# Another order of the same instructions, from the first scores on, in a fused attention and SoLU kernel

## The chip, the core and the metric

The kernel runs on one core of a Trainium2 chip. The metric is device time in microseconds (us) per execution. A program for this core is five streams of instructions that run side by side and meet at semaphores: TensorE (PE in the profile) multiplies matrices, VectorE (DVE) and ScalarE (ACT) work elementwise and read its results from PSUM, GpSimd (POOL) works on SBUF, and SyncE (SP) issues transfers. Each stream runs in the order in which it is written.

## The reference

A cluster-routed attention over 4 batches, 8 heads, 768 tokens and 64 dimensions, and a feed-forward layer with a SoLU activation and a layer norm on its 3072 tokens:

```python
def _attn_ref(q, k, v, centroids):
    q_assign = np.argmax(np.einsum('bhsd,hcd->bhsc', q_n, c_n), axis=-1)
    k_assign = np.argmax(np.einsum('bhsd,hcd->bhsc', k_n, c_n), axis=-1)
    mask = q_assign[:, :, :, None] == k_assign[:, :, None, :]
    scores = np.where(mask, scale * (q @ k.transpose(0, 1, 3, 2)), -1000000000.0)
    return softmax(scores) @ v

def _moe_ref(x, w_in, w_out, g_ln):          # x: 3072 x 512, w_in: 512 x 1024
    h = x @ w_in
    solu = h * softmax(h)
    ln = (solu - mean(solu)) / sqrt(var(solu) + 1e-06) * g_ln
    return ln @ w_out
```

Here `q_n`, `k_n` and `c_n` are rows divided by their norms, and there are 16 centroids for each head.

## The kernel before

**Attention.** The work goes by pairs of heads: 4 batches with 4 pairs each, 16 pairs in all, written b.p below (the second pair of batch 0 is 0.1). For one pair SyncE loads the rows of q and k (`raw`, L406, or L381 in a few pairs) and v (`vf`, L536). They are turned so that the dimensions lie on the partitions (`xt`: on VectorE at L414, or on TensorE at L393 with a copy at L400). TensorE multiplies them with the centroids: 8 matmuls into one PSUM buffer make a cluster-score group (`csc`, L452 and L457). VectorE takes the maximum (L479) and makes a one-hot row of the cluster (`oht`, L491 to L501). GpSimd casts q and k to bf16 (L440, L442) into the pair's place in `qk` and copies the one-hot rows beside them (L513 and L523; L532 blanks the rest), so that one product gives the score and the mask together.

There are six places (`slot`), used in turn, so copies, casts and blanks of a pair wait for the scores of the pair six before it, and the scores of a pair wait for its copies. TensorE then multiplies in banks of 512 columns (`sps`, L615, two matmuls in a bank). A bank lies in one of three PSUM buffers that are used in turn, and ScalarE's exponential (`e`, L625) empties it. A value group is six matmuls with `v` (`ops`, L644) into one of six places of an output bank. When such a bank is full, VectorE takes the reciprocal of the sums (L656) and scales (L669) into `x`. There is one such bank, so the next value group waits for that division.

**Feed-forward.** It goes by row tiles of 128 tokens, 24 in all, f = 0 to 23. SyncE transposes `x` by a transfer (L704). TensorE computes h in four parts of two 512-column matmuls (`hreg`, L736). VectorE takes the maximum (L742), ScalarE the exponential (L748), VectorE the product with h (`u`, L755). SyncE transposes `u` (L760), VectorE makes the statistics (L766, L770), GpSimd a factor alpha from them (L776, L782, L785). TensorE multiplies with the output weights (`yps`, L800, eight 512-column matmuls), and VectorE or ScalarE scales the result by alpha (L817), after which SyncE stores it (L827). `hreg` has three banks, of which even row tiles use the first two and odd ones the last two. A single PSUM buffer serves both the cluster-score groups and y, so each of these waits for whoever emptied it last.

**What sets the order.** The class `Weave` holds the whole program as operations with names, kinds and needs. `ORDER` (L28 to L78) gives for each of the five engines a list of kinds in which a number repeats the kind before it: `S` a score bank, `V` a value group, `h` one of the four parts of a row tile's h, `y` one of the parts of its y, `cl` a cluster-score group, `ca`, `cv`, `pl` and `bl` casts of q and k, casts of v, copies of one-hot rows and blanks, `al` and `at` steps of alpha, `ld` and `lv` loads, `tx`, `tu` and `ou` the transfers of x, u and the output, `ex` the exponential of h, `N` a division. `queues` takes, for each entry, the next operation of that kind that is written for that engine, so operations of one kind never pass each other:

```python
for kind, n in re.findall(r"([A-Za-z]+)(\d*)", text):
    for _ in range(int(n or 1)):
        queues[e].append(of[e, kind].pop(0))
```

`run` walks the five lists together to a plan of start times and writes the instructions out by them; what each engine runs, and in what order, is fixed by its list. `AWAY` says which operations run on another engine than their default.

Of the kernel before, what the change touches and what calls it, by code (L numbers as in the profile page):

```python
# [22 lines left out]
class Weave:  # L23
# [5 lines left out]
    ORDER["SP"] = """
        ld4 si ld4 lg lv ld2 lv ld3 lo ld lv ld2 lv ld2 lo2 ld3 lo ld4 li ld li3 tx ld lv  # L30
        ld3 lv tx ld3 tu ld8 tu tx ld5 lv tu ld3 ou ld3 tu ou ld2 lv ld10 tu ld6 ou tx lv
        ld2 tu ld ou ld2 tx ld tu ld2 lv ld2 tx ld tu ou2 ld lv ld8 tu2 ld ou ld7 pl ou ld
        lv2 ld3 tu lv tx ou tu lv pl ld4 ou2 tx lv tu tx ou tu pl2 tu2 tx tu tx ou2 tx ou tu
        tx2 ou tu2 ou2 tu2 ou6
    """
    ORDER["POOL"] = """
        po zo ca3 z ca pl ca bl pl2 ca bl ca pl sg cv z ca3 cv ca pl cv pl2 ca2 pl gs pl2 cv
        ca z ca z2 cv ca2 pl3 ca2 pl cv pl3 ca bl ca wi4 cv at ca2 pl2 cv ca pl ca pl cv al
        at2 ca cv bl ca al ca pl al pl bl pl cv at pl ca4 at ca2 al ca pl2 bl pl2 cv2 ca3 al
        at pl2 bl pl2 ca pl al ca3 at cv at pl ca pl2 ca2 pl al cv2 bl cv2 pl2 ca pl al pl  # L40
        at al at pl2 ca3 at al bl cv pl2 bl cv2 ca3 pl5 al cv3 at al ca2 cv ca cv ca2 at ca2
        pl ca al pl2 at2 pl3 at ca cv al at2 al2 at2 al at al3 at al2 at2 al2
    """
    ORDER["PE"] = """
        fl wm fl tp2 cp fl2 cl tp fl tp fl4 cl S3 tp2 S cq tp S tp S tp S2 tp S tp S2 cl S2
        tp S V S V S V S gt V S V2 S cl S3 V3 S tp S tp S tp S2 tp V S V2 S2 cl S4 V S V3 S3
        V S V S V S V S cl S3 V3 S2 V S su S4 V2 S V S V su S4 V2 S V S V me S4 V2 ptx V2 S4
        cl S2 V2 S h S V S V S h3 S2 V2 S V S2 V h2 V S V S V S h S V S h S3 V S h S V3 h S
        V2 S h S h S2 y S y2 S y S V S V S V cl h S V S h S2 V2 S h2 S3 y4 V2 h V S V S h S
        V h V S h2 S y3 S2 y V3 h S3 cl V2 S V S y S2 y2 S3 V3 S y S2 V3 S2 cl S V S2 V2 S h  # L50
        S2 V2 S V S h S2 V2 cl V2 S3 y2 S V S2 V y S2 y V2 S3 h2 S V h S h S2 V h S V S V y2
        S h V y2 S2 V S h3 S cl V S2 V2 S h V cl S3 h2 V y V S3 y2 V S h V3 S y S h S2 h2 S3
        V2 y h S V S2 y V3 y S3 h3 y S3 V3 S h S V S V cl S V S h S cl V2 S3 y V2 S y S2 y
        V2 S3 h y V S3 V h V2 S3 cl S2 V2 S y3 S2 y S V3 S V S y S2 V S V3 S2 y2 S3 y V2 S2
        h V2 S3 h3 S V S2 V y S V h2 V2 S y S2 y V y S h2 S3 cl h V S2 V3 S h V2 S3 h2 S y
        S2 V h S2 V y2 V4 S3 y h S2 h V h V S V S y2 S3 V3 h2 S2 h2 S2 y2 S V S h2 S V3 S2 h
        S h S2 V S y V2 S V y2 S2 h2 S2 h2 V2 S2 V2 y S2 h V2 h V S2 h S V h S3 V2 h y S V
        y3 V h3 S2 y3 S2 y h2 V2 h y h y3 h V h V y4 h ptx h y4 h2 y3 h2 y ptu2 y6 ptu y ptu
        y5
    """  # L60
    ORDER["DVE"] = """
        cn xa cb ca tb mx oh ot pl2 tb mx oh ot xa3 cf xa2 ca cv tb xa mx oh gk N ot pl tb
        xa mx xa oh xa ot N xt pl N tb mx xt cv N oh ot tb mx pl N oh ot ca N xt sk N ce xt
        tx ce N ce2 tb ce2 N ce hm ce N u mx bn oh N hm ot xt u bn2 ag N hm xt sc xt tb u
        bn2 N hm mx bn ag oh u ot xt ag N cv bn hm bn ag sc xt2 tb mx N u xt oh ot sc N bn2
        xt ag xt tb N hm mx tb N oh ot u xt mx N bn oh bn xt hm ot ag N cv u bn2 xt hm tb mx
        u N tb oh mx hm ot bn2 oh ag u N sc ag hm bn ot u bn N xt2 ag xt2 hm tb N bl mx tb
        bn2 oh u N xt ag xt sc hm ot tb mx oh N bn sc N u bn N ag xt ot bn ca N mx sc oh hm
        u bn ag N xt hm bn2 bl tb u ot ag N hm mx bn2 u bn N oh ot hm bl2 u ag N cv hm sc bn
        u N hm ag bn N bn u bn2 hm ag2 N bn u bn2 N ag hm bn u N ag hm bn2 u bn2 hm sc u N  # L70
        ag2 bn tx hm bn sc u bn ag hm bn tu ag u2 bn2 ag sc
    """
# [1228 lines left out]
```

## Time and profile before

| | |
|---|---|
| three runs | 223.04, 223.62, 223.04 us |
| median | 223.04 us |
| span of the profiled execution, first to last instruction | 221.0 us |
| mean granted clock of TensorE in it | 0.999 |
| instructions in it | 6580 |
| transfers | 38.67 MB, mean 175 GB/s |

The span of the profiled execution is the time from its first to its last instruction; the runs' time is taken on the device around the whole execution, and is 2.04 us above it. In the views, a row gives a source line, an engine, an operation and its tiles (out<-in, partitions x elements) with the count and the busy time. In brackets or behind a bar stands how long the engine was idle before, and what ended that time. "PEld" are TensorE's weight loads, which lie beside its matmuls, and "SPq" are SyncE's issues. The lines themselves stand in the prediction where they are used.

### The profile page before, as it was taken

Reading aid. Unit: us, or ns where it says so; the run is one execution under the profiler, and the core shown is the slowest. Engines: PE = TensorE matmul, PEld = TensorE weight load, DVE = VectorE, ACT = ScalarE, POOL = GpSimd, SP = SyncE. Lnnn points to the kernel's source line nnn. Section 1 sums busy time; section 2 is a strip of 40 time slices with the busy share of each in tenths; the row PEclk is TensorE's granted clock in tenths of the full one; section 3 lists DMA queues with packets and bytes.
Section 4 is the critical chain, followed back from the end, with each engine's and each line's share of the span. In section 5 each row is a group of like instructions: output and inputs, shape, how many; then the busy total and the mean of one; then the engine's idle time right before and its main releaser. Section 6 shows DMA issues by size and latency. Waiting matters only on the chain.

```text
span 221.0 us, 6580 instructions
## 1 busy us (share of the span) xinstructions
PE 213.4 (97%) x2392; PEld 148.3 (67%) x2424; DVE 197.3 (89%) x356; ACT 191.0 (86%) x372; POOL 130.1 (59%) x251
## 2 busy tenths in 40 slices
PE   7999999999999999999999999999999999999993
PEld 4667766767766687775677776777677677755452
DVE  3899998999999999998998989887999889888982
ACT  2799999989988999998899899999899998983363
POOL 3699989933845999637667634953895403022331
PEclk9999999999999999999999999999999999999999
DMA  6999988979999979999999896599930434396723
GB/s 147 346 279 236 281 197 223 274 159 164 176 175 209 192 157 141 204 215 176 202 221 162 189 177 169 123 210 208 237 59 19 89 63 130 90 134 169 176 78 142
DMA packets 125167, 38.67 MB, mean 175 GB/s; under 512 B 114504, under 2 KB 120656, under 8 KB 125136
## 3 DMA queue, kind: packets, MB, share of 16 engines
q1 hardware_dynamic: 123392, 37.73, 82.5%
q10 hardware_dynamic: 1744, 0.52, 1.0%
q8 instruction: 19, 0.31, 0.6%
q14 instruction: 12, 0.10, 0.1%
HBM read 23.11 MB, written 6.29 MB: 133 GB/s over the span
## 4 chain that ended last, share of the span: by engine, by line
PE 88%; DMA 3%; ACT 2%; DVE 2%; issue 2%; POOL 0%; ACTq 0%; DVEq 0%
PE sps L615 27%; PE yps L800 17%; PE hreg L736 16%; PE ops L644 15%; PE csc L457 4%; DMA uT<-u 3%; PE hreg L393 2%; ACT e L625 2%; PE idle_p L844 1%; PE hreg L615 1%; PE csc L452 1%; PE hreg L583 1%; PE hreg L800 1%; DVE u L755 1%; PE hreg L593 0%
## 5 line engine op out<-in xcount | busy, mean ns | idle before, releaser
L625 ACT ACTIVATE e<-sps 128x512 bf16<-128x512 f32 (+1 forms) x278 | 144.4, 609 | 9.6 <-PE sps L615 8.4
L615 PE MATMUL sps<-qk 80*128 80x256 bf16 (+5 forms) x616 | 92.4, 264 | 0.6 <-DVE qk L523 0.3
L615 PEld LDWEIGHTS <-qk 80*128 80x128 bf16 (+1 forms) x636 | 60.3, 121 | 25.7 <-issue 8.0
L644 PEld LDWEIGHTS <-e 128*128 128x128 bf16 x1134 | 50.0, 97 | 12.0 <-issue 1.9
L644 PE MATMUL ops<-v,e 128*128 128x65 bf16 x1134 | 55.0, 193 | 0.1
L736 PE MATMUL hreg<-w_in_sb,xT 128*128 128x512 bf16 x172 | 48.9, 379 | 1.2 <-issue 0.2
L800 PE MATMUL yps<-w_out_c,uT 128*128 128x512 bf16 x172 | 46.5, 379 | 0.9 <-DMA uT<-u 0.4
L523 POOL COPY qk<-oht 32x384 f32<-32x384 f32 (+1 forms) x48 | 24.0, 500 | 16.2 <-DVE oht L501 14.1
L755 DVE TENSOR_TENSOR u<-e_sb,hreg 128x1024 bf16<-128x1024 bf16 (+1 forms) x25 | 29.2, 1170 | 4.4 <-ACT e_sb L748 4.2
L748 ACT ACTIVATE e_sb<-hreg,nmax 128x1024 bf16<-128x1024 f32 x24 | 27.0, 1124 | 5.8 <-DVE nmax L742 5.7
L742 DVE TENSOR_REDUCE nmax<-hreg 128x1 f32<-128x1024 f32 x24 | 29.1, 1211 | 3.0 <-PE hreg L736 2.8
L766 DVE BATCH_NORM_STATS2 bs<-u 128x6 f32<-128x512 bf16 x48 | 31.5, 678 | 0.1
L800 PEld LDWEIGHTS <-uT 128*128 128x128 bf16 x200 | 18.3, 97 | 12.2 <-DMA uT<-u 0.5
L440 POOL CAST qk<-xt 64x768 bf16<-64x768 f32 (+1 forms) x30 | 24.4, 814 | 3.2 <-DVE xt L400 1.7
L442 POOL TENSOR_SCALAR qk<-xt 64x768 bf16<-64x768 f32 (+1 forms) x31 | 25.1, 809 | 2.0
L782 POOL TENSOR_SCALAR esq<-es,mv 128x1 f32<-128x1 f32 x24 | 8.7, 362 | 29.3 <-DVE mv L770 21.3
L736 PEld LDWEIGHTS <-xT 128*128 128x128 bf16 x192 | 16.7, 97 | 10.3 <-issue 1.3
L414 DVE STREAM_TRANSPOSE xt<-raw 128x768 f32<-128x768 f32 x24 | 22.6, 952 | 0.0
L669 DVE TENSOR_TENSOR x<-ops,den 128x256 bf16<-128x256 f32 (+1 forms) x39 | 18.9, 486 | 1.3
L776 POOL TENSOR_SCALAR es<-esum 128x1 f32<-128x1 f32 x24 | 5.3, 222 | 25.1 <-ACT e_sb L748 24.7
L541 POOL CAST v<-vf 128x384 bf16<-128x384 f32 x27 | 13.9, 528 | 5.6 <-DMA vf<-in_v_dram 4.9
L785 POOL TENSOR_TENSOR alpha<-esq,halves 128x1 f32<-128x1 f32 x24 | 13.7, 570 | 2.0
(86 smaller groups left out, 186.2 us busy)
## 6 DMA issues: line engine op xcount, KB each, us to landing
vf<-in_v_dram SPq DMA_DIRECT2D x16, 384.0 KB, 5.2
out_dram<-y SPq DMA_DIRECT2D x23, 256.0 KB, 2.6
raw<-in_q_dram SPq DMA_DIRECT2D x50, 96.0 KB, 3.5
raw<-in_k_dram SPq DMA_DIRECT2D x50, 96.0 KB, 3.5
w_g<-in_moe_w_out_dram SPq DMA_DIRECT2D x4, 512.0 KB, 6.5
w_st<-in_moe_w_in_dram SPq DMA_DIRECT2D x4, 512.0 KB, 5.8
raw<-in_q_dram SPq DMA_DIRECT2D x3, 384.0 KB, 6.1
raw<-in_k_dram SPq DMA_DIRECT2D x3, 384.0 KB, 6.6
```

Of the source, the lines that this page charges most:

```text
L440: VEC[e].tensor_copy(dst, src)
L442: VEC[e].tensor_scalar(dst, src, scalar1=inv_C, scalar2=1.0, op0=Alu.mult, op1=Alu.mult)
L523: ins = VEC[e].tensor_copy(dst.bitcast(F32), src.bitcast(F32).unsqueeze(1) .to_broadcast([NB, 2, n // 2]))
L615: ins = nc.tensor.matmul(sps_[n, k][:, c0:c0 + w], side(b, h // 2, 1, h % 2, keys)[r], side(b, h // 2, 0, h % 2, slice(s0 * P, s0 * P + w) ...
L625: ins = nc.scalar.activation(es[n, k][:, :w], sps_[n, k][:, :w], Act.Exp, scale=exp_scale, bias=-exp_scale)
L644: nc.tensor.matmul(opss[g][:, s, :VW], es[n, k][:, c0:c0 + P], v1[slot(b, h // 2)][:, h % 2, kt, :VW], start=(kt == 0), stop=(kt == n_t - 1))
L736: uses(nc.tensor.matmul(hreg[:, at(f, f2)[1], :], xTs[f][:, dc, :], w_in_sb[:, dc, f2 * FF2:(f2 + 1) * FF2], start=(dc == 0), stop=(dc == ...
L742: uses(nc.vector.tensor_reduce(ff[f, "nmax"][:], pair_of(f), axis=AXY, op=Alu.max, negate=True), *both(f))
L748: uses(nc.scalar.activation(ff[f, "e"][:], pair_of(f), Act.Exp, bias=ff[f, "nmax"][:], accum_out=ff[f, "esum"][:]), *both(f))
L755: uses(nc.vector.tensor_tensor(ff[f, "u"][:, at_], ff[f, "e"][:, at_], pair_of(f)[:, at_], op=Alu.mult), *banks)
L766: nc.vector.bn_stats(ff[f, "bs"][:, f2, :], ff[f, "u"][:, f2, :])
L800: ins = nc.tensor.matmul(dst, ff[f, "uT"][:, at(f, f2)[0] * (n_fc // 2) + c, :], w_out_c[:, fc, cols], start=(fc == chunks[0]), stop=(fc = ...
```

## The change

The five lists of `ORDER` are replaced. Each new list has every operation of the old one exactly as often (733 entries for TensorE, 307 for VectorE, 348 for ScalarE, 216 for GpSimd, 196 for SyncE). `AWAY`, the buffers, the types and every function that writes an instruction are the same. TensorE's list is as it was up to the first three score banks, and the others up to about the same time: the first entry that differs is the 17th of SyncE, the 11th of GpSimd, the 22nd of TensorE, the 21st of VectorE and the 15th of ScalarE.

```diff
     ORDER["SP"] = """
-        ld4 si ld4 lg lv ld2 lv ld3 lo ld lv ld2 lv ld2 lo2 ld3 lo ld4 li ld li3 tx ld lv
+        ld4 si ld4 lg lv ld2 lv ld2 lo ld2 lv ld2 lv ld2 lo ld2 lo ld2 lo ld2 li ld2 li3 ld
...
     ORDER["POOL"] = """
-        po zo ca3 z ca pl ca bl pl2 ca bl ca pl sg cv z ca3 cv ca pl cv pl2 ca2 pl gs pl2 cv
+        po zo ca3 z ca pl ca bl ca z pl3 ca bl cv ca2 z ca sg pl2 ca2 cv pl cv ca3 pl2 gs pl
...
     ORDER["PE"] = """
-        fl wm fl tp2 cp fl2 cl tp fl tp fl4 cl S3 tp2 S cq tp S tp S tp S2 tp S tp S2 cl S2
+        fl wm fl tp2 cp fl2 cl tp fl tp fl4 cl S3 tp cq tp S2 tp2 S tp S2 tp S cl S2 tp S tp
...
```

In TensorE's list the value groups, which stood alone 75 times, in twos 34 times, in threes 15 times and in a four once, stand alone 19 times, in twos 17 times, in threes 22 times, in fours 14 times and in longer runs three times. TensorE goes from a value group straight to a score bank 31 times instead of 87.

Three places are shown, each first as it was and then as it is. The first is TensorE at about 52 us, the second half of a row tile's h (row tile 1) and the three score banks behind it. Names carry buffer numbers here, which differ between two programs: a new number of `sps` is a new bank.

```order
L736 LDWEIGHTS xT_981
L736 MATMUL hreg_111<-w_in_sb_112,xT_981 128x512
L736 LDWEIGHTS xT_981
L736 MATMUL hreg_111<-w_in_sb_112,xT_981 128x512
L615 LDWEIGHTS qk4_103
L615 MATMUL sps_1259<-qk4_103 128x256
L615 LDWEIGHTS qk4_103
L615 MATMUL sps_1259<-qk4_103 128x256
L615 LDWEIGHTS qk4_103
L615 MATMUL sps_1266<-qk4_103 128x256
```

```order
L615 MATMUL sps_1259<-qk4_103 128x256
L615 LDWEIGHTS qk4_103
L615 MATMUL sps_1259<-qk4_103 128x256
L736 LDWEIGHTS xT_1034
L736 MATMUL hreg_111<-w_in_sb_112,xT_1034 128x512
L736 LDWEIGHTS xT_1034
L736 MATMUL hreg_111<-w_in_sb_112,xT_1034 128x512
L615 LDWEIGHTS qk4_103
L615 MATMUL sps_1270<-qk4_103 128x256
```

The first part of the next row tile's h (it reads another transposed x, `xT_1034`) has come in between the first and the second of the three score banks; before, the three followed each other.

The second is SyncE at about 92 us, around the transpose of u of row tile 5:

```order
L704 DMA_TRANSPOSE xT<-x 128x8x128
L536 DMA vf<-in_v_dram 128x2x384
L406 DMA raw<-in_k_dram 32x24x32 x2
L760 DMA_TRANSPOSE uT<-u 128x8x128
L406 DMA raw<-in_k_dram 32x24x32
L827 DMA out_dram<-y 128x512
```

```order
L704 DMA_TRANSPOSE xT<-x 128x8x128
L406 DMA raw<-in_q_dram 32x24x32
L760 DMA_TRANSPOSE uT<-u 128x8x128
L406 DMA raw<-in_q_dram 32x24x32
L406 DMA raw<-in_k_dram 32x24x32 x3
L536 DMA vf<-in_v_dram 128x2x384
```

Between the transpose of x and that of u stands one load where three stood, and the value load has gone behind both.

The third is GpSimd at about 31 us, around the copies of one-hot rows for pair 0.3 (`qk_102<-w_out_c`):

```order
L541 CAST v_3_108<-vf 128x6x64
L442 TENSOR_SCALAR qk_102<-xt 64x6x128 x2
L513 COPY qk_102<-w_out_c 16x2x3x64 x3
L440 CAST qk_103<-xt 64x768 x2
L523 COPY qk_103<-oht 32x2x192
L541 CAST v_3_108<-vf 128x6x64
```

```order
L442 TENSOR_SCALAR qk_102<-xt 64x6x128 x2
L1266 MEMSET v_4_109 128x12x8
L440 CAST qk_103<-xt 64x768 x2
L541 CAST v_3_108<-vf 128x6x64 x2
L513 COPY qk_102<-w_out_c 16x2x3x64 x3
L442 TENSOR_SCALAR qk_103<-xt 64x768
```

The two casts of the next pair (`qk_103`) and the value casts now stand ahead of the three copies.

More of the change, by code (lines that the diff above doesn't have):

```diff
@@ L29 @@
     ORDER["SP"] = """
-        ld4 si ld4 lg lv ld2 lv ld3 lo ld lv ld2 lv ld2 lo2 ld3 lo ld4 li ld li3 tx ld lv
[L31 to L34, printed above, removed]
+        ld4 si ld4 lg lv ld2 lv ld2 lo ld2 lv ld2 lv ld2 lo ld2 lo ld2 lo ld2 li ld2 li3 ld
@@ L35 @@
+        lv ld2 tx2 ld2 lv ld2 tu ld tx ld4 lv2 ld tu ld4 tu ld ou ld2 lv ld2 tu ld8 ou ld2
+        ou ld4 tu ld2 ou ld4 tx ld tu ld4 lv ld tx ld tu ld3 ou lv tu ld6 ou ld tx ld6 lv ld
+        tu ld3 lv pl ou ld3 tu lv ld tu ou ld ou ld2 lv ld2 tx ld tu ld lv ou pl2 ou tx tu2
+        tx ou tu pl tx tu tx tu ou2 tx tu ou tx tu ou tx ou tu2 ou tu ou6
     """
     ORDER["POOL"] = """
-        po zo ca3 z ca pl ca bl pl2 ca bl ca pl sg cv z ca3 cv ca pl cv pl2 ca2 pl gs pl2 cv
-        ca z ca z2 cv ca2 pl3 ca2 pl cv pl3 ca bl ca wi4 cv at ca2 pl2 cv ca pl ca pl cv al
@@ L39 @@
[L39 to L42, printed above, removed]
+        po zo ca3 z ca pl ca bl ca z pl3 ca bl cv ca2 z ca sg pl2 ca2 cv pl cv ca3 pl2 gs pl
+        cv ca2 z ca2 cv2 pl3 ca pl wi ca wi3 pl3 bl at ca2 cv2 pl2 bl ca pl2 al ca cv at cv
@@ L43 @@
+        ca cv z ca2 al pl at pl3 at bl al ca2 cv ca2 cv al ca at pl3 bl pl al cv pl4 bl at
+        ca pl2 al ca pl ca5 at pl bl al ca3 cv pl2 ca4 cv pl cv pl at al at cv2 ca at ca pl
+        al ca pl bl at pl cv pl ca pl cv ca al ca cv pl cv pl2 ca cv pl2 at cv al bl pl at
+        ca pl ca al at cv ca al ca pl ca pl al pl ca2 cv pl at3 al at al at2 al3 at al2 at2
+        al2 at al
     """
     ORDER["PE"] = """
-        fl wm fl tp2 cp fl2 cl tp fl tp fl4 cl S3 tp2 S cq tp S tp S tp S2 tp S tp S2 cl S2
@@ L46 @@
[L46 to L57, printed above, removed]
@@ L58 @@
-        y3 V h3 S2 y3 S2 y h2 V2 h y h y3 h V h V y4 h ptx h y4 h2 y3 h2 y ptu2 y6 ptu y ptu
-        y5
+        fl wm fl tp2 cp fl2 cl tp fl tp fl4 cl S3 tp cq tp S2 tp2 S tp S2 tp S cl S2 tp S tp
+        S2 V tp S2 V5 gt S3 cl S3 V3 S tp S2 tp S2 tp S V3 S2 cl S3 V3 S V S4 V2 S2 V2 S cl
+        S V S3 V3 S2 su S4 V3 S2 V S su S2 V2 S3 V2 S2 me S3 V4 ptx S4 cl S2 V4 S2 h S2 h3
+        S2 V2 S V S V h S V h S V S V2 S h S2 h S h S2 V2 h S V4 S2 y2 S2 y h S h S2 y S V3
+        h S h S2 V3 cl S h S h S2 h S y S h y S V4 S y S V y S3 V h y S h S y S y S V3 y S3
@@ new lines @@
+        h V3 cl S2 V2 h S2 y S y S2 h S V4 S3 y2 S2 h S V2 S2 cl S2 V3 S2 V cl S V4 S2 y S y
+        S2 V y S2 y S V3 S3 h2 S V4 h S2 h S y S V y h S h S2 y2 S2 h2 S2 V3 cl S2 V2 h S cl
+        S h S2 h S V3 h S3 V3 S y S2 y2 S2 V3 y h S h S2 V3 h S2 h S y S2 y S V4 h S3 V h y
+        S2 V h y S3 h cl S2 V2 cl h S3 V4 y2 S3 y S h y S3 V6 h S3 cl S2 h S y S y2 S y V4
+        S2 y S2 V4 S2 y S y S y S2 V4 S2 h S h S2 h2 S2 V3 h S h V3 y S y S2 y S y S h2 S3
+        V4 cl S2 h2 S V2 h S3 h2 S2 V y S2 V2 h S2 y S y V3 y S2 h2 S h S2 y S h S V6 y S y
@@ L60 @@
+        S3 h2 S2 V S h V3 h S y S V2 S2 h2 S2 y S2 V2 h S h y S V3 S2 h2 S2 y V y S2 h S V h
+        S V3 h2 S y S2 h y2 S h V4 y h S h S y S y2 h y h S V2 y h2 y3 h S h y4 V2 h2 y2 ptx
+        y2 h2 y3 h2 y ptu2 y6 ptu y ptu y5
     """
     ORDER["DVE"] = """
-        cn xa cb ca tb mx oh ot pl2 tb mx oh ot xa3 cf xa2 ca cv tb xa mx oh gk N ot pl tb
-        xa mx xa oh xa ot N xt pl N tb mx xt cv N oh ot tb mx pl N oh ot ca N xt sk N ce xt
-        tx ce N ce2 tb ce2 N ce hm ce N u mx bn oh N hm ot xt u bn2 ag N hm xt sc xt tb u
@@ L65 @@
[L65 to L70, printed above, removed]
@@ L71 @@
-        ag2 bn tx hm bn sc u bn ag hm bn tu ag u2 bn2 ag sc
+        cn xa cb ca tb mx oh ot pl2 tb mx oh ot xa3 cf xa2 tb cv mx xa oh ot gk N pl tb xa
+        mx xa oh ca xa ot N xt pl tb N mx xt oh N cv ot tb ca mx oh N pl ot N xt sk N xt ce2
+        tx N ce4 N ce2 hm tb N u mx bn N xt hm oh bn ot u N bn xt ag hm xt sc u N tb bn mx
+        ag hm cv bn oh bn u ot bn2 xt N xt ag2 hm sc N tb mx u xt oh bn ot N bn xt sc hm xt
+        tb cv N mx tb N oh ag ot u mx xt N bn xt oh N bn hm ag ot xt u bn2 xt hm tb ag mx oh
@@ L72 @@
+        u N bn tb mx hm N bn ot xt u oh ag bn sc xt N hm bn bl ot u xt N xt bn ag tb hm mx
+        tb mx oh ot u N bn xt2 sc N ag oh tb hm bn2 sc N ag u mx ot N bn oh xt N bn ot ca hm
+        sc ag xt N u bn2 bl hm u tb mx bl N oh ag hm bn ot bn u cv ag bn2 hm N bl u N bn ag
+        hm bn N u sc hm N ag u bn2 hm N bn u bn hm ag N bn u N bn hm bn2 u ag2 bn ag hm sc
+        bn u bn N ag hm tx sc u bn2 ag hm bn tu u ag u bn2 ag sc
     """
     ORDER["ACT"] = """
-        wa xa3 pl ca E2 xa E8 pl E6 xa E11 xa E49 ex E10 ex E6 ca E4 ex E8 ex E3 sc E5 ca E2
@@ L75 @@
-        ex E25 ex E9 sc E6 ex E5 sc E2 ex E9 ex E8 ex E9 sc E6 ex E18 ex E21 ex E5 sc E3 ex
-        E9 ex E7 sc E2 ex E7 ex E8 ex E7 ex E6 sc E ex E2 sc E3 ex E2 sc ex sc ex sc ex tu
-        sc tu2 sc2 oz
+        wa xa3 pl ca E2 xa E5 pl E7 xa E13 xa E49 ex E11 ex E5 ca E4 ex E8 ex E4 sc E5 ca E3
+        ex E22 ex E13 sc E4 ex E4 sc E3 ex E13 ex E11 ex E5 sc E5 ex E16 ex E19 ex E6 sc E2
+        ex E11 ex E5 sc E3 ex E8 ex E8 ex E7 ex E2 sc E4 ex E sc E3 ex sc E2 ex E sc ex sc
+        ex tu sc tu2 sc2 oz
```

## The prediction

> **What bounds the kernel now.** I read the page's busy shares and its chain of waits first. They say which engine the end hangs on.
>
> ```profile
> PE 213.4 (97%) x2392; PEld 148.3 (67%) x2424; DVE 197.3 (89%) x356; ACT 191.0 (86%) x372; POOL 130.1 (59%) x251
> PE 88%; DMA 3%; ACT 2%; DVE 2%; issue 2%; POOL 0%; ACTq 0%; DVEq 0%
> ```
>
> TensorE holds 88% of the chain, and no other engine more than 3%. Next come the windows: busy time of each engine in stretches of the span, then granted clock, DMA share and GB/s.
>
> ```profile
> core 0: us, PE busy (x) PEld busy (x) DVE busy (x) ACT busy (x) POOL busy (x), PEclk, DMA share, GB/s
> 0.00:8.90 8.90, 7.35 (x44) 4.27 (x44) 4.90 (x20) 3.42 (x7) 4.67 (x20) 1.00 0.78 213
> 20.00:40.00 20.00, 19.98 (x278) 14.27 (x276) 18.36 (x36) 19.79 (x42) 18.16 (x31) 1.00 0.99 248
> 40.00:60.00 20.00, 19.61 (x225) 14.08 (x226) 19.63 (x34) 19.40 (x40) 12.11 (x19) 1.00 1.08 183
> 217.80:221.00 3.20, 0.00 (x0) 0.00 (x0) 0.48 (x1) 0.21 (x1) 0.00 (x0) 0.92 0.42 149
> ```
>
> The span less TensorE's busy time is 221.0 - 213.4 = 7.6 us. The stretch ahead of the first scores holds 8.90 - 7.35 = 1.55 of it and the last scaling with its store 3.20, so only 2.85 us of visible idle time lies in the 208.9 us between. But a matmul's recorded end is modelled, so a short wait can hide inside "busy". The honest measure is the work itself, counted by groups and priced by pieces of the chain in which matmuls follow each other without a gap (start, us, what).
>
> ```profile
> L625 ACT ACTIVATE e<-sps 128x512 bf16<-128x512 f32 (+1 forms) x278 | 144.4, 609 | 9.6 <-PE sps L615 8.4 <-PE ops L644 0.2
> L644 PE MATMUL ops<-v,e 128*128 128x65 bf16 x1134 | 55.0, 193 | 0.1
> L736 PEld LDWEIGHTS <-xT 128*128 128x128 bf16 x192 | 16.7, 97 | 10.3 <-issue 1.3 <-DVE u L755 0.5 <-DVE w_out_c L596 0.2
> L800 PEld LDWEIGHTS <-uT 128*128 128x128 bf16 x200 | 18.3, 97 | 12.2 <-DMA uT<-u 0.5 <-issue 0.3
> 9.60 0.66 PE hreg L393 x6
> 18.77 0.55 PE ops L644 x18
> 28.50 0.78 PE csc L457 x8
> 30.59 0.44 PE sps L615 x4
> 66.25 1.73 PE yps L800 x8
> ```
>
> A score bank (two matmuls) takes 0.22 us and there is one per exponential: 278 here and 16 more into other tiles, so 294 x 0.22 = 64.7. A value matmul takes 0.55/18 = 0.031: 1152 (1134 and 18 from another tile) give 35.2. A 512-column matmul takes 1.73/8 = 0.216: 192 at L736 and 184 at L800 (16 of its 200 loads serve half-width matmuls) give 81.2. Fifteen cluster-score groups after the first scores take 15 x 0.78 = 11.7, 36 transposes 36/6 x 0.66 = 4.0, and smaller pieces not shown about 4. The sum is 201 us in a stretch of 209. So **about 8 us** is all that any order of this work could win, and part of it cannot go. In those 20 us windows ScalarE is busy for 19.79 and 19.40 and VectorE for 18.36 and 19.63: three engines are near full, and the order decides which of them stands still for a moment.
>
> **The change, part by part.** No instruction is added or removed, so each term is a place where TensorE stands still now, or might stand still next.
>
> *Term 1, scores that outrun the exponentials, 47 to 56 us.* Timeline of TensorE (start, us, engine, line, op, count):
>
> ```profile
> 47.28 0.79 PE L615 MATMUL sps<-qk 80*128 80x256 bf16 x4
> 47.91 0.35 PE L644 MATMUL ops<-v,e 128*128 128x65 bf16 x6
> 52.10 1.10 PE L615 MATMUL sps<-qk 80*128 80x256 bf16 x6
> 53.04 0.35 PE L644 MATMUL ops<-v,e 128*128 128x65 bf16 x6
> 54.18 0.71 PE L644 MATMUL ops<-v,e 128*128 128x65 bf16 x18
> 54.94 0.38 PE L736 MATMUL hreg<-w_in_sb,xT 128*128 128x512 bf16 x1
> 55.38 0.38 PE L615 MATMUL sps<-qk 96*128 96x256 bf16 x2
> ```
>
> Four score matmuls from 47.28 should end at 47.72, and the next work starts at 47.91: 0.19 lost. Six from 52.10 should end at 52.76, next 53.04: 0.28. Eighteen value matmuls from 54.18 end at 54.73, two 512-column ones at 55.16 (one record is missing), next 55.38: 0.22. The sum is 0.69. The score banks are a ring of three, and each waits for the exponential three banks back. In the new order a half of a row tile's h product (0.43 us) stands between the first and second of the three banks at 52 us, value groups stand ahead of the scores at 55 us, and a value group and an h half ahead of the last scores at 47 us. What they bring forward is ready: the x transpose that the moved h needs is queued on SyncE right behind the one before it. The gain lies between 0 (the wait returns at the next ScalarE detour) and 0.69; each hole is covered by pieces longer than itself, so I take **-0.6**.
>
> *Term 2, the y matmuls that wait for a transposed u, 99 us.* TensorE, then SyncE's issues:
>
> ```profile
> 98.77 0.35 PE L644 MATMUL ops<-v,e 128*128 128x65 bf16 x6
> 99.52 1.04 PE L800 MATMUL yps<-w_out_c,uT 128*128 128x512 bf16 x4 [0.40 <-DMA uT<-u]
> 92.21 0.53 SPq L536 DMA_DIRECT2D vf<-in_v_dram  x1
> 92.79 1.03 SPq L406 DMA_DIRECT2D raw<-in_k_dram  x2
> 93.92 2.14 SPq L760 DMA_TRANSPOSE uT<-u  x1
> ```
>
> Six value matmuls from 98.77 end at 98.95, so y stands still for 0.57 us. SyncE spent 1.56 us on a value load and two key loads just ahead of that transpose; afterwards one load is left there. That brings the issue about 1 us forward, while the new list asks for these y matmuls about 0.9 us of TensorE work earlier and puts ten VectorE instructions instead of five between the maximum and the product of that row tile, whose h in turn comes about 3 us earlier. The first two cancel; the last two nearly do. From 0 (all of the wait stays) to -0.57: I take **-0.4**.
>
> *Term 3, a cluster-score group behind a late scaling, 156 us.*
>
> ```profile
> 155.96 0.82 PE L615 MATMUL sps<-qk 96*128 96x256 bf16 x6
> 156.90 0.85 PE L457 MATMUL csc<-xt,c_bd 128*32 128x384 f32 x8
> ```
>
> Six score matmuls end at 156.62; the group starts 0.28 later, because it needs the bank that a scaling frees. The new list puts four value groups (0.7 us) ahead of it. From 0 to -0.28: **-0.2**.
>
> *Term 4, GpSimd ahead of the fourth pair's scores, 32 us.* GpSimd, with TensorE's scores at 32.39:
>
> ```profile
> 31.14 1.72 POOL L513 COPY qk<-w_out_c 16x384 f32<-16x384 f32 x3 [0.39 <-DVE w_out_c L498]
> 32.39 0.83 PE L615 MATMUL sps<-qk 80*128 80x256 bf16 x6
> 32.93 1.92 POOL L440 CAST qk<-xt 64x768 bf16<-64x768 f32 x2
> 35.79 0.50 POOL L541 CAST v<-vf 128x384 bf16<-128x384 f32 x1
> ```
>
> The two casts at 32.93 and the value cast at 35.79, 2.4 us together, now stand ahead of the three copies, of which the scores need two. Two of three copies end about 0.2 us ahead of those scores now. If GpSimd had no room, it would be 2.4 - 0.39 (its wait) - 0.2 = 1.8 us late, and everything on TensorE behind it. But the first copies of the second pair have 1.2 us less ahead of them, so the queue gets here with a lead, and the copies wait for L498 in any case. From 0 to +1.8, nearer to the lower end: **+0.3**.
>
> *Term 5, a blank that loses its lead, 150 us.*
>
> ```profile
> 138.44 0.41 POOL L532 MEMSET qk<- 16x384 f32 x1
> 150.02 0.61 PE L615 MATMUL sps<-qk 80*128 80x256 bf16 x4
> L440 POOL CAST qk<-xt 64x768 bf16<-64x768 f32 (+1 forms) x30 | 24.4, 814 | 3.2 <-DVE xt L400 1.7 <-ACT xt L400 0.2
> L669 DVE TENSOR_TENSOR x<-ops,den 128x256 bf16<-128x256 f32 (+1 forms) x39 | 18.9, 486 | 1.3
> ```
>
> The scores that read its result are the second bank of the row at 150.02, 11.4 us later. In the new GpSimd list 18 instructions come ahead of it, 15 of them from later (about 11.5 us at 0.77 each, near the means of the casts), one of them an alpha chain that waits for VectorE. The lead is gone. From 0 to +0.8 (the length of one cast that happens to wait): **+0.2**.
>
> Everything else I cost at nothing. What hides it: at most boundaries between two output banks, where VectorE's division must fit, more TensorE work now stands than before (in the two orders of TensorE 23 of 38 boundaries have more between them than before, 13 less), and the loads keep their order of urgency. If that cover fails at one boundary, the price is one division: the 0.49 us of L669 and its reciprocal.
>
> Sum: -0.6 - 0.4 - 0.2 + 0.3 + 0.2 = -0.7 us, so a span of 220.3. The median of the runs shown is 223.04, 2.04 above the profiled span: **222.3 us**, that is 0.3% less. A measurement of this kernel can tell about 0.3% (0.67 us) from no change, so the forecast lies just at that bound.
>
> **The places in TensorE's list that no hole marks.** Value groups, which alternated with scores, now come in runs of three and four. Each run lets the exponentials catch up, so the ring of three banks is filled later and emptied more evenly; this is where a gain could come that I have not counted.
>
> **Rivals.**
> *More is won (220.1).* The loss is 8 us and I account for 1.5 of it. If the runs of value groups even out a quarter of the rest too, 1.6 us, and terms 1 to 3 come in full (1.5) against 0.2 of cost: 223.04 - 1.6 - 1.5 + 0.2 = 220.1. For it: 40:60, where TensorE lost most, has both ScalarE and VectorE at 97% or more, so evenness matters there. Against it: beyond those above I find no wait of TensorE in its timeline that passes 0.25 us.
> The Trainium skill, "Perfetto Trace Analysis", section "Identifying the Most-Contended Engine", says that matmul busy time is a poor measure and weight-load busy time a better one; by that rule 67% leaves a third of the span to win. The count above disagrees: 201 of 209 us is matmul issue, and no order shortens it.
> *Nothing is won (223.0).* ScalarE at 19.79 of 20 us is the next wall: what the scores do not wait for at 52 us they wait for at 60. For it: the windows. Against it: ScalarE's idle time is 9.6 us ahead of exponentials, mostly waiting for scores, so there is slack to trade.
> *Slower (225.0).* GpSimd comes late. Its list has been packed so that copies and blanks stand just ahead of their scores, and it runs in order. Its durations are not steady (min/median/max ns):
>
> ```profile
> L523 POOL COPY qk<-oht x48: 339/501/818, 8.5 to 170.3; 32x384 f32<-32x384 f32 x44, 32x192 f32<-32x192 f32 x4
> L442 POOL TENSOR_SCALAR qk<-xt x31: 503/827/1075, 6.2 to 172.2; 64x768 bf16<-64x768 f32 x27, 64x384 bf16<-64x384 f32 x4
> ```
>
> At the long ends a cast costs 0.25 more and a copy 0.32 more. Five casts and three copies ahead of the scores at 32 us make 2.2 us; with the lead of 0.2 used up, 2.0 us reach TensorE: 225.0. It decides from the point at which the last copy ends more than 0.2 us after TensorE gets there. For it: GpSimd is busy for 18.16 of the 20 us from 20 to 40. Against it: from 40 to 60 its share is 12.11 of 20, and most of its copies stand there.
> The Trainium skill, "GPSIMD Engine Reference", section "1. Specifications", says that GpSimd shares its SBUF interfaces with VectorE and contends with two-input VectorE instructions; that would be a reason for the long ends, and it speaks against packing.
>
> **How the numbers follow.** The forecast has 0.42 (0.60 of it faster by over 0.3%, 0.35 within, 0.05 slower), more won 0.16, nothing won 0.12 (0.10, 0.60, 0.30), slower 0.30. Faster: 0.25 + 0.16 + 0.01 = 0.42. Within 0.3%: 0.15 + 0.07 = 0.22. Slower: 0.02 + 0.04 + 0.30 = 0.36. The forecast's own range goes from all gains and no cost (-1.54: 221.5) to half of the gains with the costs as taken (-0.1: 222.9). The range for 8 in 10 takes in the first two rivals and the third as far as 224.8: 220.2 to 224.8.
>
> **What would show it.** Right: no gap ahead of the scores near 52 and 55 us, no wait of L800 on uT near 99 us, the copies of L513 ending ahead of the scores near 32 us. Wrong: weight loads of L615 that wait for GpSimd copies by more than 0.5 us in total (term 4 or the third rival), TensorE standing still for ScalarE between 56 and 130 us (second rival), or y matmuls that wait for uT at other places than 99 us, which would say that SyncE's list, which I price at one place only, decides.

## The result, and the profile after

| | before | changed |
|---|---|---|
| median of 22 runs each, same chip | 223.02 us | 223.81 us |
| ratio, with its 95% interval | | 1.0033 (1.0017 to 1.0050) |
| again, on another occasion, 35 runs and 12 | 223.06 us | 223.65 us, 1.0032 (1.0008 to 1.0057) |
| span of the profiled execution | 221.0 us | 221.8 us |

The change makes the kernel 0.3% slower, 0.8 us, where 0.7 us less was forecast. The ratios, and the times of the experiments below, leave out executions that ran over 1.5% above the fastest of the same kernel. First the page of the changed kernel: busy shares and the chain of waits.

```profile
PE 213.1 (96%) x2394; PEld 147.9 (67%) x2424; DVE 198.7 (90%) x356; ACT 192.2 (87%) x372; POOL 129.6 (58%) x251
PE 76%; DVE 11%; DMA 5%; issue 2%; SPq 2%; POOL 1%; ACT 1%; DVEq 0%; ACTq 0%; POOLq 0%
```

TensorE's share of the chain has fallen from 88% to 76%, and VectorE, which had 2%, holds 11%. Such a share follows one chain of one execution: in two traces of a faster kernel below TensorE has 85% and 63%. So it is a hint, and the windows, in the columns of the prediction, say where to look:

```profile
core 0: us, PE busy (x) PEld busy (x) DVE busy (x) ACT busy (x) POOL busy (x), PEclk, DMA share, GB/s
20.00:40.00 20.00, 18.53 (x257) 12.62 (x255) 18.07 (x34) 18.58 (x39) 17.09 (x27) 1.00 1.01 261
40.00:60.00 20.00, 19.69 (x238) 14.04 (x240) 19.00 (x34) 19.40 (x40) 9.72 (x17) 1.00 0.90 153
```

From 20 to 40 us TensorE was busy for 19.98 us and is now for 18.53. From 40 to 60 us, where it stood still most, it has gone from 19.61 to 19.69. Here is that first window on the timeline of the changed kernel, TensorE's rows that waited and GpSimd's rows around the copies of the fourth pair:

```profile
27.58 0.54 PE L644 MATMUL ops<-v,e 128*128 128x65 bf16 x12 [0.64 <-DVE x L669]
29.61 1.82 POOL L440 CAST qk<-xt 64x768 bf16<-64x768 f32 x2
30.81 0.36 PE L644 MATMUL ops<-v,e 128*128 128x65 bf16 x6 [0.55 <-DVE v L541]
31.50 0.95 POOL L541 CAST v<-vf 128x384 bf16<-128x384 f32 x2
32.52 2.05 POOL L513 COPY qk<-w_out_c 16x384 f32<-16x384 f32 x3
32.74 1.06 PE L583 MATMUL hreg<-w_g,w_out_c 128*32 128x512 f32 x8
33.96 0.82 PE L615 MATMUL sps<-qk 80*128 80x256 bf16 x6
35.74 0.39 PE L615 MATMUL hreg<-qk 80*128 80x256 bf16 x2 [0.23 <-DVE qk L513]
```

Three waits for VectorE come one after the other: for a scaling, for a value cast, for a copy. GpSimd's copies of the fourth pair start at 32.52 instead of 31.14 and have no idle time before them any more. The scores that need the first two (33.96) start within 0.2 us of the second one's end. So two engines are late by about the same time, and this view can't say which of them sets it.

Behind 40 us the places of terms 2, 3 and 5 look like this (TensorE):

```profile
99.22 0.39 PE L615 MATMUL sps<-qk 80*128 80x256 bf16 x2
99.44 0.60 PE L800 MATMUL yps<-w_out_c,uT 128*128 128x512 bf16 x2
99.87 0.38 PE L615 MATMUL sps<-qk 80*128 80x256 bf16 x2
...
150.10 1.03 PE L736 MATMUL hreg<-w_in_sb,xT 128*128 128x512 bf16 x4
150.96 0.60 PE L615 MATMUL sps<-qk 80*128 80x256 bf16 x4
151.40 0.71 PE L644 MATMUL ops<-v,e 128*128 128x65 bf16 x18
...
157.94 0.89 PE L644 MATMUL ops<-v,e 128*128 128x65 bf16 x24
158.76 0.85 PE L457 MATMUL csc<-xt,c_bd 128*32 128x384 f32 x8
```

The y matmuls follow the scores at once (0.22 us for two score matmuls), near 150 us nothing stands still, and the cluster-score group comes 0.08 us behind 24 value matmuls (24 x 0.031 = 0.74) instead of 0.28 behind its scores.

All holes together, by the prices of the prediction (the time between neighbouring score and value matmuls less the work that lies between them), in us; the last two columns are runs told of below. The sums hang on the prices, the differences between columns much less so.

| window | before | changed | changed, second trace | changed, GpSimd's piece as before |
|---|---|---|---|---|
| 9 to 20 us | 0.62 | 0.52 | 0.54 | 0.52 |
| 20 to 30 us | 1.03 | 2.22 | 1.13 | 1.57 |
| 30 to 40 us | 0.37 | 0.89 | 3.89 | 0.36 |
| 40 to 60 us | 1.75 | 1.06 | 1.04 | 1.07 |
| 60 to 90 us | 1.10 | 0.96 | 0.88 | 1.04 |
| 90 to 100 us | 0.73 | 0.23 | 0.30 | 0.14 |
| 100 to 140 us | 1.35 | 1.91 | 1.98 | 1.38 |
| 140 to 205 us | 1.97 | 1.27 | 1.30 | 1.27 |
| sum | 8.9 | 9.1 | 11.1 | 7.4 |

So the new order wins 1.4 to 1.5 us behind 40 us and gives 1.7 us or more back between 20 and 40. The first two columns differ by less than the spans do, because the first scores started at 9.42 us in this trace and at 8.95 in the one before, in code that is the same (below).

### The profile page after: what moved, and what is told of

It reads as the page before. It is cut to its first block, busy times and chain, and to the rows that moved or that the text cites. A ratio compares the mean times of both kernels' runs of the same rounds, so it can differ in the third digit from the quotient of the medians.

```text
span 221.8 us, 6593 instructions
## 1 busy us (share of the span) xinstructions
PE 213.1 (96%) x2394; PEld 147.9 (67%) x2424; DVE 198.7 (90%) x356; ACT 192.2 (87%) x372; POOL 129.6 (58%) x251
## 4 chain that ended last, share of the span: by engine, by line
PE 76%; DVE 11%; DMA 5%; issue 2%; SPq 2%; POOL 1%; ACT 1%; DVEq 0%; ACTq 0%; POOLq 0%
PE sps L615 23%; PE yps L800 17%; PE hreg L736 16%; PE ops L644 12%; PE csc L457 3%; DMA raw<-in_k_dram 3%; DMA vf<-in_v_dram 2%; DVE cst L466 1%; PE hreg L393 1%; DVE xt L414 1%; DVE mx L479 1%; DVE nmax L742 1%; SPq L406 1%; DVE oh L491 1%; DVE w_out_c L498 1%
## 5 line engine op out<-in xcount | busy, mean ns | idle before, releaser
L615 PE MATMUL sps<-qk 80*128 80x256 bf16 (+5 forms) x616 | 91.1, 263 | 0.6 <-DVE qk L523 0.3
L615 PEld LDWEIGHTS <-qk 80*128 80x128 bf16 (+1 forms) x636 | 63.6, 120 | 37.8 <-issue 9.3
L736 PE MATMUL hreg<-w_in_sb,xT 128*128 128x512 bf16 x173 | 50.8, 379 | 1.3 <-issue 0.2
L800 PE MATMUL yps<-w_out_c,uT 128*128 128x512 bf16 x173 | 49.0, 379 | 0.4
L644 PE MATMUL ops<-v,e 128*128 128x65 bf16 x1134 | 47.2, 193 | 1.4 <-DVE x L669 0.6
L644 PEld LDWEIGHTS <-e 128*128 128x128 bf16 x1134 | 44.0, 97 | 5.5 <-DVE x L669 1.3
L523 POOL COPY qk<-oht 32x384 f32<-32x384 f32 (+1 forms) x48 | 23.4, 487 | 17.0 <-DVE oht L501 11.1
L442 POOL TENSOR_SCALAR qk<-xt 64x768 bf16<-64x768 f32 (+1 forms) x31 | 25.7, 829 | 2.4 <-ACT xt L400 0.5
```

What stands on the lines that cost most here:

```text
L442: VEC[e].tensor_scalar(dst, src, scalar1=inv_C, scalar2=1.0, op0=Alu.mult, op1=Alu.mult)
L615: ins = nc.tensor.matmul(sps_[n, k][:, c0:c0 + w], side(b, h // 2, 1, h % 2, keys)[r], side(b, h // 2, 0, h % 2, slice(s0 * P, s0 * P + w) ...
L644: nc.tensor.matmul(opss[g][:, s, :VW], es[n, k][:, c0:c0 + P], v1[slot(b, h // 2)][:, h % 2, kt, :VW], start=(kt == 0), stop=(kt == n_t - 1))
L736: uses(nc.tensor.matmul(hreg[:, at(f, f2)[1], :], xTs[f][:, dc, :], w_in_sb[:, dc, f2 * FF2:(f2 + 1) * FF2], start=(dc == 0), stop=(dc == ...
L800: ins = nc.tensor.matmul(dst, ff[f, "uT"][:, at(f, f2)[0] * (n_fc // 2) + c, :], w_out_c[:, fc, cols], start=(fc == chunks[0]), stop=(fc = ...
```

## The experiments

All times are medians; each ratio is against runs of the kernel before on the same chip. These took 223.16, 222.92 and 223.04 us on the three occasions, so ratios compare better than times. Each list entry is a kind and a count, as in the description of `ORDER`.

### The two halves of the change: before 40 us and behind it

First, the old order up to 40 us and the new one behind it, in all five lists. VectorE's list at the seam:

```diff
         xa mx xa oh xa ot N xt pl N tb mx xt cv N oh ot tb mx pl N oh ot ca N xt sk N ce xt
-        tx ce N ce2 tb ce2 N ce hm ce N u mx bn oh N hm ot xt u bn2 ag N hm xt sc xt tb u
+        ce tx N ce4 N ce2 hm tb N u mx bn N xt hm oh bn ot u N bn xt ag hm xt sc u N tb bn
...
```

> The old order for everything that started before 40 us, the new order for the rest. Theory E (the loss lies between 20 and 40 us, where the new order costs TensorE 1.6 us more, and the places after 40 us gain 1.4): 1.4 us less than before, about 221.6 us, and TensorE's idle time after 40 us about 5.4 us instead of 6.9. Rival R1 (the later order gains nothing of its own, it only takes up again what it lost before): 223.0 us. Rival R2 (the later order itself is the slower one): 223.8 us or more.

And the new order up to 40.5 us with the old one behind it; VectorE's list at its start:

```diff
-        cn xa cb ca tb mx oh ot pl2 tb mx oh ot xa3 cf xa2 ca cv tb xa mx oh gk N ot pl tb
-        xa mx xa oh xa ot N xt pl N tb mx xt cv N oh ot tb mx pl N oh ot ca N xt sk N ce xt
+        cn xa cb ca tb mx oh ot pl2 tb mx oh ot xa3 cf xa2 tb cv mx xa oh ot gk N pl tb xa
+        mx xa oh ca xa ot N xt pl tb N mx xt oh N cv ot tb ca mx oh N pl ot N xt sk N xt ce
...
```

> The new order for everything that started before 40.5 us, the old order for the rest. Theory E: before + 1.6, about 224.6 us (225.1 if the first scores start 0.47 us late again). Rival R1: 223.8 us, as the whole change. Rival R2: 223.0 us.

The early half alone took 225.0 us, 1.0079 of before (1.0048 to 1.0109): theory E's 224.6 to 225.1. Its own trace has holes of 0.35, 0.43 and 1.27 us ahead of the value groups at 27 and 30 us and of the scores at 34 us, the last of them a wait for GpSimd. Four of its twelve runs had a mean granted clock of 0.990 to 0.992 and took 226.1 to 226.4 us; the median of the other eight is 224.5. The late half alone took 222.9 us, 0.998 (0.996 to 1.001), where theory E had 221.6. Its profiled execution holds a standstill of 1000 us, so the trace to read is that of a repetition:

> The old order up to 40 us and the new one behind it, once more, since its first profile holds a standstill of 1000 us that no other run has. The first time gave 0.998 of before. If the holes that the new order closes after 40 us are worth their length, TensorE's idle time after 40 us is 5.4 us against 6.9 and the time 1.0 to 1.4 us less than before (221.8 us). If not, new holes of 1 us in sum stand elsewhere after 40 us, and the time is 0.2 to 0.4 us less (222.7 us).

222.9 us, 1.0002 (0.998 to 1.002). TensorE's holes behind 40 us add up to 5.5 us, as the theory had it, but the median did not fall. (The profiled execution itself did gain: its first scores started at 9.71 us and its span is 220.7 us, so it took 211.0 us from there on, against 212.1 before.) So the loss lies ahead of 40 us. What the late half is worth is less sure: with the new early half in front it is 1.0079 less 1.0033, 0.46% or 1.0 us, or about 0.6 us when the runs with a lower clock are left out on both sides; with the old one in front 0 to 0.4 us by the ratios.

### VectorE or GpSimd, starting from the changed kernel

Three pieces of VectorE's list as before, in the changed kernel:

```diff
-        mx xa oh ca xa ot N xt pl tb N mx xt oh N cv ot tb ca mx oh N pl ot N xt sk N xt ce2
+        mx xa oh ca xa ot N xt pl N tb mx xt cv N oh ot tb ca mx pl N oh ot N xt sk N xt ce2
```

> The changed kernel with three places of VectorE's list between 25 and 35 us as before: the second, third and fourth scaling of an output bank, one value cast and one copy of a one-hot row go ahead of a transpose, a one-hot comparison and a comparison again. Theory V (TensorE's holes at 26.6, 29.9 and 35.2 us, 0.80 + 0.73 + 0.40, come from this list alone): 1.9 us less than the change, about 221.9 us. Rival G (GpSimd's copies of the fourth pair end at 33.8 us in any case, so the scores behind them take over the wait): only what lies behind them, 0.4 us, is won: 223.4 us, with a new hole ahead of the scores near 33 us.

It took 223.57 us, 1.0003 (0.998 to 1.002): rival G's 223.4, not theory V's 221.9. Against the change that is 0.2 us less by the medians and 0.7 by the ratios, whose intervals overlap. Its trace shows the wait changing hands. TensorE and GpSimd:

```profile
26.64 0.53 PE L644 MATMUL ops<-v,e 128*128 128x65 bf16 x12
30.31 0.71 PE L644 MATMUL ops<-v,e 128*128 128x65 bf16 x18
32.79 1.85 POOL L513 COPY qk<-w_out_c 16x384 f32<-16x384 f32 x3
33.92 0.81 PE L615 MATMUL sps<-qk 80*128 80x256 bf16 x6 [1.14 <-POOL qk L513]
```

The value groups at 26 and 30 us show no wait any more, and the scores at 33.92 wait 1.14 us for GpSimd's copies, which start at 32.79, no earlier than in the change (32.52).

Then also GpSimd's piece as before (and in a further run that piece alone, with VectorE's list as changed):

```diff
-        cv ca2 z ca2 cv2 pl3 ca pl wi ca wi3 pl3 bl at ca2 cv2 pl2 bl ca pl2 al ca cv at cv
+        cv ca2 z pl3 ca2 cv2 ca pl wi ca wi3 pl3 bl at ca2 cv2 pl2 bl ca pl2 al ca cv at cv
```

> The kernel with VectorE's three places as before, and in GpSimd's list also the three copies of the fourth pair ahead of two casts of the fifth pair and two value casts, as before. Theory V: the same as without GpSimd's part, about 221.9 us. Rival G: only now are the 1.9 us won, 221.9 us, where VectorE's part alone gave 223.4. If neither wins over 0.5 us, the loss from 20 to 40 us has another cause.

> The changed kernel with GpSimd's piece alone as before (three copies of the fourth pair ahead of two casts and two value casts), VectorE's list as changed. If the two engines are late side by side, either alone gives little: 0 to 0.4 us less than the change, 223.4 to 223.8 us, with the holes of 0.8 and 0.7 us at 26.6 and 29.9 us left. If GpSimd alone decides: 222.6 us, as with both pieces.

Both pieces together: 222.61 us, 0.998 (0.996 to 1.001). GpSimd's piece alone: 222.03 us, 0.9974 (0.9946 to 1.0002). Moving three copies ahead of four casts takes the whole loss away, and VectorE's pieces add nothing to it that can be seen. Of the two answers expected, the one came in which GpSimd alone decides. The trace of GpSimd's piece alone, chain of waits and timeline:

```profile
PE 85%; DVE 10%; DMA 1%; issue 1%; SPq 1%; DVEq 0%
...
30.84 1.84 POOL L513 COPY qk<-w_out_c 16x384 f32<-16x384 f32 x3 [0.90 <-DVE w_out_c L498]
31.81 1.06 PE L583 MATMUL hreg<-w_g,w_out_c 128*32 128x512 f32 x8
32.75 1.97 POOL L440 CAST qk<-xt 64x768 bf16<-64x768 f32 x2
33.04 0.82 PE L615 MATMUL sps<-qk 80*128 80x256 bf16 x6
```

The copies now wait 0.90 us for their input, start at 30.84 and are done before the scores; the casts behind them keep nobody waiting.

To settle whether that gain holds, it was run once more, beside the change itself:

> The changed kernel with GpSimd's piece as before, once more, beside the change itself. If its first result holds: 0.997 of before, 222.2 to 222.4 us, and 1.3 to 1.8 us less than the change. If that was luck of seven runs: 223.0 us and 0.8 less than the change.

> The change itself, on the same chip as the three others. 1.003 of before, 223.6 us, if its first result holds. In its trace the scores of the fourth pair (32 to 34 us) start when GpSimd's second copy ends, within 0.2 us, and the first scores of the program between 8.8 and 9.7 us, as in the traces so far.

222.45 us, 0.9961 (0.9935 to 0.9988), against 223.65 us, 1.0032. The piece is worth 1.2 us, and without it the change is faster than both kernels. The second trace of the change itself (span 223.0) shows the wait open. It is not a typical one: its mean granted clock is 0.992, and 3 of the change's 34 runs have 0.991 or 0.992. In it the first scores started at 8.65 us, 0.77 earlier than in the first trace. TensorE, GpSimd and the windows behind:

```profile
30.85 1.07 PE L583 MATMUL hreg<-w_g,w_out_c 128*32 128x512 f32 x8
31.85 0.39 PE L615 MATMUL hreg<-qk 80*128 80x256 bf16 x2
33.00 1.64 POOL L513 COPY qk<-w_out_c 16x384 f32<-16x384 f32 x3
34.13 0.82 PE L615 MATMUL sps<-qk 80*128 80x256 bf16 x6 [1.89 <-POOL qk L513]
```

```profile
32.00:34.00 2.00, 0.25 (x2) 0.10 (x1) 1.67 (x5) 0.83 (x2) 1.88 (x4) 1.00 1.12 248
34.00:36.00 2.00, 1.87 (x29) 1.63 (x29) 0.00 (x0) 1.39 (x3) 1.80 (x4) 0.88 1.15 244
36.00:38.00 2.00, 2.00 (x17) 0.67 (x15) 1.41 (x3) 1.65 (x4) 0.11 (x1) 0.50 1.13 207
```

The copies start at 33.00, half a microsecond later than in the first trace, though the first scores began earlier: GpSimd's own work sets their time. From its first cast to these copies it was busy for 24.85 us here and for 23.82 in the first trace, with the same instructions. What was hidden behind a late start and VectorE in the first trace is a hole of 1.89 us here. And after it the granted clock (third number from the right) falls to 0.50.

### The same pieces put into the kernel before

```diff
-        ca z ca z2 cv ca2 pl3 ca2 pl cv pl3 ca bl ca wi4 cv at ca2 pl2 cv ca pl ca pl cv al
+        ca z ca z2 cv ca4 cv pl7 ca bl ca wi4 cv at ca2 pl2 cv ca pl ca pl cv al at2 ca cv
...
```

> The kernel before, with one piece of GpSimd's list changed as in the new order: two casts of the fifth pair and one value cast go ahead of the three copies of the fourth pair (at 31 us). Theory G (GpSimd has no lead to spend here; its 2.4 us less its idle 0.39 and its lead of 0.2 reach TensorE): a hole of 1.3 to 1.8 us ahead of the scores at 32.4 us and 1.0 to 1.8 us more time, 224.1 to 224.9 us. Rival, as forecast: the lead covers most of it, 0.3 us, 223.4 us.

Of GpSimd's piece, three casts ahead of the copies: 226.34 us, 1.0144 (1.0111 to 1.0176), or 3.2 us. That is more than either theory's bound. The trace says why (TensorE, then the windows):

```profile
34.43 1.25 PE L615 MATMUL sps<-qk 80*128 80x256 bf16 x6 [2.00 <-POOL qk L513]
```

```profile
34.00:36.00 2.00, 1.57 (x10) 1.15 (x10) 1.28 (x3) 1.07 (x3) 1.84 (x4) 0.66 0.88 150
36.00:38.00 2.00, 2.00 (x28) 1.74 (x27) 0.00 (x0) 1.70 (x4) 1.83 (x4) 0.50 0.94 268
```

The wait itself is 2.0 us, as theory G had it. Then the clock falls to 0.50 for some 3 us, and six score matmuls that took 0.83 us take 1.25.

With one cast of the three:

```diff
-        ca z ca z2 cv ca2 pl3 ca2 pl cv pl3 ca bl ca wi4 cv at ca2 pl2 cv ca pl ca pl cv al
+        ca z ca z2 cv ca3 pl3 ca pl cv pl3 ca bl ca wi4 cv at ca2 pl2 cv ca pl ca pl cv al
```

> The kernel before, with only one cast (0.8 us) of the fifth pair ahead of the three copies of the fourth pair in GpSimd's list, where three of them (2.4 us) made 3.2 us. If the price grows with the lateness beyond the lead (0.8 less 0.4 idle less 0.2), 0.2 to 0.5 us and no drop of the granted clock: 223.2 to 223.4 us. If any piece ahead of the copies costs its whole length: 223.8 us.

223.3 us, 1.001 (0.999 to 1.003): the lateness beyond the lead, not the whole cast. The trace has it directly, a wait of 0.46 us:

```profile
31.98 1.73 POOL L513 COPY qk<-w_out_c 16x384 f32<-16x384 f32 x3
33.20 0.82 PE L615 MATMUL sps<-qk 80*128 80x256 bf16 x6 [0.46 <-POOL qk L513]
```

VectorE's three pieces alone, in the kernel before:

```diff
-        xa mx xa oh xa ot N xt pl N tb mx xt cv N oh ot tb mx pl N oh ot ca N xt sk N ce xt
+        xa mx xa oh xa ot N xt pl tb N mx xt oh N cv ot tb mx oh N pl ot ca N xt sk N ce xt
```

> The kernel before, with three pieces of VectorE's list between 25 and 34 us changed as in the new order: a transpose or a one-hot comparison goes ahead of the second, third and fourth scaling, of one value cast and of one copy. Theory V (VectorE's order is a cost of its own): holes ahead of the value groups at 26.4 and 29.9 us (0.5 and 0.6) and of the scores at 33 us (1.1), 1.2 to 2.2 us more, 224.2 to 225.2 us. Rival G alone: TensorE takes it up within 10 us, since GpSimd's copies set the time at 32 us: under 0.4 us, 223.5 us.

223.73 us, 1.0039 (1.0020 to 1.0058), between the two theories. Of the three places only one costs anything: no hole has come at 26 and 30 us, and one ahead of the scores behind the late copy.

```profile
32.26 0.83 PE L615 MATMUL sps<-qk 80*128 80x256 bf16 x6
33.76 0.38 PE L615 MATMUL hreg<-qk 80*128 80x256 bf16 x2 [0.67 <-DVE qk L513]
```

### Term 1 by itself

TensorE's list alone, at 47 to 56 us, in the kernel before:

```diff
-        cl S2 V2 S h S V S V S h3 S2 V2 S V S2 V h2 V S V S V S h S V S h S3 V S h S V3 h S
+        cl S2 V2 S h S V S V S h3 S2 V2 S V S V h S h V S V S V S h S V S h S h S2 V2 h S V2
...
```

> The kernel before, with TensorE's list alone changed at 47 to 56 us as term 1 describes it: a value group and half of an h part ahead of the scores at 47.7 us, a part of the next row tile's h between the first and second score bank at 52 us, value groups and an h part ahead of the scores at 55 us. Term 1 as forecast: the three holes of 0.19, 0.28 and 0.22 us are gone, 0.4 to 0.7 us less, 222.4 us. Rival (nothing is won, ScalarE is the next wall): holes of the same sum move to 50 to 60 us, 223.0 us.

223.43 us, 1.0023 (0.9998 to 1.0049): nothing is won, as the rival had it. The hole at 52 us is gone, and two others have come. TensorE and ScalarE:

```profile
48.84 0.60 PE L736 MATMUL hreg<-w_in_sb,xT 128*128 128x512 bf16 x2 [0.43 <-DVE w_out_c L596]
49.33 5.10 ACT L625 ACTIVATE e<-sps 128x512 bf16<-128x512 f32 x10
56.06 0.38 PE L615 MATMUL sps<-qk 96*128 96x256 bf16 x2 [0.49 <-ACT e L625]
```

The part of h that was brought forward waits 0.43 us for VectorE, and ScalarE goes through ten exponentials without a break, so the scores wait 0.49 us behind its next exponential of h. The holes from 40 to 60 us sum to 1.87 us, against 1.75 before and 1.06 in the whole change. The gain there is seen in both traces of the whole change, so it comes from the lists of several engines that moved together, not from TensorE's alone. It is not steady: in the second trace of the kernel with GpSimd's piece put back, the same windows hold 1.6 us again.

## Why the prediction was wrong, point by point

**What bounds the kernel, and the 8 us.** Right, and a little low: 24 of the 294 score banks are 384 columns wide, not 512, which takes 1.3 us off the work by its columns and makes the sum 9. The holes are 8.9 us, the new order can move them about, and the best version measured here (GpSimd's piece put back) has 7.4 us in one trace and 8.6 in another.

**Term 4 is the step that failed**: "But the first copies of the second pair have 1.2 us less ahead of them, so the queue gets here with a lead". The place, the mechanism and the upper bound's arithmetic (2.4 less 0.39 less 0.2) were right, and it was then taken at 0.3 because of that lead. The lead wasn't there. The windows from GpSimd's first cast to these copies, before and changed, in the columns of the prediction (GpSimd is the fifth engine):

```profile
5.64:31.14 25.50, 25.06 (x315) 18.04 (x313) 23.65 (x51) 23.71 (x54) 21.93 (x41) 1.00 1.00 266
5.64:32.52 26.88, 25.29 (x315) 17.73 (x314) 24.92 (x52) 23.71 (x54) 23.82 (x44) 1.00 1.02 270
```

GpSimd's work ahead of the copies grew by 1.9 us (two casts of q and k and one of v more, one short memset less), and its idle time fell by 0.5 in all, the wait of 0.39 at the copies, subtracted already, among it; so the copies came 1.4 us later. In an engine that runs in order, an instruction starts at the sum of the work listed ahead of it and of the waits in between. Putting some of that work in another order among itself changes nothing for what comes behind, unless a wait goes: the second pair's copies did start 1.4 us earlier (17.67 against 19.08), but what was moved from ahead of them stands behind them. In the second trace the fourth pair's copies came 1.9 us late (33.00 against 31.14). In the changed kernel that costs 1.2 us by the runs made side by side. In the old order three casts cost 3.2, and 2.1 to 2.2 in the two runs whose clock did not fall. So the upper bound of 1.8 was too low as well, and the larger part of what it left out goes with the clock after a wait of that length.

**The third rival (GpSimd late, 225.0)** named the mechanism and the point from which it decides, and had 0.30. It should have had most of the chance: the row of 18.16 busy of 20 us, quoted for it, left little room for a lead. Its size, 2.0, was that of the bare hole; the median shows 1.2, perhaps because VectorE is late at the same time, as in the first trace, which the runs don't settle.

**Term 1 (-0.6).** The size agrees with the changed kernel (1.75 to 1.06 from 40 to 60 us), the reason does not: the moves on TensorE alone won nothing.

**Term 2 (-0.4).** The wait is gone (0.73 to 0.23 from 90 to 100 us). But it was partly chance: in five other kernels of this study with the old order at that place the same hole was 0.1 to 0.3 us, not 0.57.

**Term 3 (-0.2).** Right: 0.28 us became 0.08.

**Term 5 (+0.2).** Nothing came of it: no hole stands there in the changed kernel.

**"Everything else I cost at nothing", with the price of one division.** At two boundaries TensorE waited for VectorE, near 27 and 30 us: 0.64 us for a scaling and 0.55 for a value cast listed behind a division. The price was about right, and the count of boundaries that grew or shrank did not show it; it leaves out how much VectorE has listed ahead of the division. Put back, VectorE's three pieces bring 0.2 to 0.7 us while GpSimd is late behind them, and nothing that can be seen when it is not. In the kernel before, the same pieces cost 0.9 us (1.0039), and there the hole stood at the third, the copy.

**The forecast as a whole** (222.3) is what the change gives without that piece of GpSimd's list: 222.03 and 222.45 us. The terms other than the fourth sum to -1.0, and these runs are 0.6 to 0.9 us below the kernel before. Whether its late half alone is worth the 1.4 us that the holes say stays open: the ratios with the old early half in front show 0 to 0.4 us, and why its runs spread wider (221.7 to 225.1 us) was not tried.

## What to carry to other kernels

For an engine with little idle time, an instruction's start is nearly the sum of the work listed ahead of it: compare these sums for the instructions that somebody waits for, and don't expect a lead from work that was only put in another order. When two engines are late at one place, a view shows the one that came last; repair one alone and see whether the wait changes hands. A hole found on one engine may only move if the lists of the engines that feed it stay as they are, as term 1 did by itself.
